# Block sums in place, fewer converted blocks and new step points in a one-core attention and bilinear-GLU kernel

## The chip, the cores and the metric

The kernel runs on one core of one Trainium2 chip. The metric is the device time of one execution in microseconds (us); lower is better. The core has five engines that run their own instruction queues: TensorE (PE, with its weight loads shown apart as PEld), VectorE (DVE), ScalarE (ACT), GpSimd (POOL) and SyncE (SP), whose queue here issues the DMA transfers.

## The reference

Input x has 2048 rows of 576 float32 numbers. All of it, cut to what matters:

```
xn = layernorm(x)
s  = attention(xn, wqkv, wo)      # 32 heads of 18, causal, window of 256
h  = (xn @ w_gate) * (xn @ w_up)  # 576 -> 4608, no nonlinearity
g  = silu(h @ w_down)             # 4608 -> 576
return x + s * g
```

## The kernel before

**Numbers in two halves.** Each float32 operand of a matmul is scaled and split into a float16 high part and a float16 low part. `hi` (line 190) makes the high part on ACT, `lo` (line 193) the low part on DVE. A product takes three matmuls: high by high, high by low, low by high.

**Seven products for eight.** The gate and up products of a group of F are done by a scheme of seven block products (Strassen's kind). A group `g` covers 256 columns of F, as F tile 0 and F tile 1 of 128 each; a chunk `c` is 512 rows of x, as two halves of 256. K (576) is four blocks of 128 and a tail of 64, block 4. The weights of gate and up (`kind` 0 and 1) come as raw float32 tiles `RAW[g, kind]` of 5 K blocks by 256 columns. `t_sum` (lines 494 to 507, on POOL) forms the differences of weight blocks that the scheme needs into a float32 tile `tf`; `t_hi` and `t_lo` split them into the float16 tile `tw`, one for each kind and each pair of sums. `up_hi` and `up_lo` split the plain blocks into `upw` tiles (`UW[g, k]`: k is 0 and 1 for F tile 0 of gate and up, 2 and 3 for F tile 1). `wd_sum`, `wd_hi` and `wd_lo` do the tail difference. `s_steps` forms the sums of x blocks once for each chunk, before and during the first slots.

**Slots and places.** There are 18 groups by 4 chunks, 72 slots: slot 4g + c does chunk c of group g. A slot has 16 places. At each place PE gets some matmuls of the seven products (`seven_place`, line 1160), and then every step that the table `AT` puts at that place is issued, in that order, to its engine. Nothing reorders an engine's queue afterwards, so the table is the order of the work. Places of a group's weight steps count from slot 4g - 4, the first slot of the group before: 0 to 15 lie in that slot, 48 to 63 in slot 4g - 1, and 64 and above in slot 4g itself, the first that uses the weights.

A slot's products come in the order 0, 2, 1, 3, 4, 5, 6. Product 2 (from place 2 of the slot) and 3 read `tw` of pair 0, products 4 (from place 9) and 5 read `tw` of pair 1, product 6 (from place 14) reads F tile 1. Results go from PSUM to SBUF on ACT and DVE (`gt`, lines 1126 and 1130); `seven_mult` (line 1135) multiplies gate by up on POOL (`ht`) or DVE; `h_hi` and `h_lo` (lines 1002 and 1008) split the product into `hh`; `down` (line 1024), one slot later, multiplies by w_down, and DVE adds it to `acc` (line 1031).

**Attention** for two heads of one chunk runs beside it in slots 1 to 64: `score_pairs` (PE), `score` (DVE, line 908), `shifted` and `probs` (ACT, lines 916 to 923), `turn_probs` (line 929: a subtraction on POOL or DVE as the table `en` says, then a transposing DMA from `pp` to `pt`), `weigh` (PE, line 941), `finish`, and a store. In slots 1 to 16 (chunk 0) there are fewer key blocks.

**Buffers.** `up_ring` gives six `upw` tiles, four a group; `tw` has four, `tf` two (also used by `ffn_spread_in`, which brings a scale back over all partitions, and by `s_steps`); `wd` one; `dn_ring` four.

**Raw loads** (`ffn_raw`) go out on SP's queue, on which the attention's loads and transposes stand too. `ffn_amax` finds the largest value (ACT squares, line 315), `ffn_spread_out`, `ffn_spread_in` and `ffn_scale` make the scale that the conversions need.

Of the kernel before, what the change touches and what calls it, by code (L numbers as in the profile page):

```python
# [8 lines left out]
F32 = mybir.dt.float32  # L9
# [11 lines left out]
def kernel(  # L21
# [43 lines left out]
    C_OUT = 1.0 / (XS * PROJ * WTOP * WTOP)  # L65
    LEAST, MOST = 2.0 ** -60, 2.0 ** 60

    AT = {"amax": (19, 20, 6),
           "dn": ((41, 45), (51, 52), (52, 48)),
           "down": ((6, 9, 12, 15, 20), (6, 8, 11, 14, 16), (6, 8, 11, 14, 16), (6, 9, 12, 15, 19)),  # L70
           "en": ((0, 1, 0, 0, 0, 0, 1, 0, 0, 0), (0, 1, 0, 0, 0, 0, 1, 0, 0, 0),
                  (0, 1, 0, 0, 0, 0, 1, 0, 0, 0), (0, 1, 0, 0, 0, 0, 1, 0, 0, 0)),
           "end": ((30, 32, 35), (28, 32, 33), (28, 32, 33), (28, 32, 33)),
           "eng": (1, 1, 0, 1, 1, 0, 1, 0, 0, 0, 0, 0, 0, 1),
           "g0": (-22, -19, -22, -21, -9, -16, -14, -11, -11),
           "h": (((15, 17), (18, 21)), ((15, 17), (19, 21)), ((15, 17), (21, 21)), ((15, 17), (19, 21))),
           "load": (8, 3, 15),
           "mult": {1: 6, 4: 18, 5: 1, 6: 0},
# [12 lines left out]
           "pairs": (6, 13),  # L91
           "raw": (8, 9, 12, 16, -6, 0),
           "scale": (26, 28, 35, 51),
           "sum": ((30, 36, 50, 59, 64), (41, 53, 56, 61, 62)),
# [5 lines left out]
           "t_hi": ((57, 57), (67, 69)),  # L100
           "t_lo": ((57, 58), (70, 71)),
           "u0": ((-9, -8, -7, -7), (-7, -7, -7, -4)),
           "up_hi": (36, 36, 60, 61),
           "up_lo": (41, 40, 65, 62),
           "wd": ((55, 56), (65, 69), (70, 74)),
           "wd0": ((-4, 3), (-1, 4), (-1, 7))}

    ctx.enter_context(tc.manual_schedule())
    const = ctx.enter_context(tc.tile_pool(name="const", bufs=1))
# [22 lines left out]
    sig = const.tile([128, 4], F32, name="sig")  # L132

    def up_ring():
        return ring.tile([128, 10, 128], F16, name="upw", bufs=6)

    def dn_ring():
        return ring.tile([128, 3, D], F16, name="dnw", bufs=4)
# [50 lines left out]
    def hi(w, rv, s):  # L189
        nc.scalar.activation(w, rv, AF.Copy, scale=s)  # L190
# [165 lines left out]

    def qk_split(m):
        if m < QM:
            w = UW["q", m] = up_ring() if m < 6 else pro.tile([128, 10, 128], F16, name=f"wq{m}")
# [76 lines left out]
    def ffn_spread_in(g):  # L436
        if g == 0:
            SC[g, "sp"] = spread_in(f"f{g}", pro, 3)
            return
        t = sums.tile([128, 2, 2, 128], F32, name="tf", bufs=2).rearrange("p a b n -> p (a b n)")  # L440
        t = t[:, 0:384].rearrange("p (a n) -> p a n", n=3)
# [12 lines left out]
    def ffn_scale2(g):  # L454
# [2 lines left out]
        nc.gpsimd.tensor_scalar(sc[:, 9:10], sc[:, 9:10], C_FFN * (FTOP / 2) ** 3, None, op0=OP.mult)  # L457
        nc.gpsimd.tensor_tensor(sc[:, 9:10], sc[:, 9:10], sc[:, 5:6], op=OP.mult)

    def up_hi(g, k):  # L460
        if (g, k) not in UW:
            UW[g, k] = up_ring()
        w = UW[g, k]
        hi(w[:, 0:5], RAW[g, k % 2][:, :, k // 2 * 128:k // 2 * 128 + 128], SC[g][:, 6 + k % 2:7 + k % 2])

    def up_lo(g, k):
        w = UW[g, k]
        lo(w[:, 5:10], RAW[g, k % 2][:, :, k // 2 * 128:k // 2 * 128 + 128], SC[g][:, 6 + k % 2:7 + k % 2],
           w[:, 0:5])

    TF, TW, SX, XD, WD = {}, {}, {}, {}, {}


    def wd_part(g, kind, i):
        if g not in WD:
            WD[g] = ring.tile([128, 2, 2, 128], F16, name="wd", bufs=1)
        return WD[g][:, i, kind]  # L480

    def wd_sum(g, kind):
        r = RAW[g, kind][:, 4]
# [10 lines left out]
    def t_sum(g, kind, n):  # L494
        r = RAW[g, kind].rearrange("p k (f n) -> p k f n", f=2)
        b = {(k, f): r[:, 2 * k:2 * k + 2, f] for k in range(2) for f in range(2)}
        if n == 0:
            if g == 0:
                TF[g, kind] = rqk.rearrange("p k n -> p (k n)")[:, 1024 * kind:1024 * kind + 1024] \
                    .rearrange("p (a k n) -> p a k n", a=4, k=2)  # L500
            else:
# [5 lines left out]
        nc.gpsimd.tensor_tensor(t[:, to], x0, x1, op=OP.subtract)  # L507

    def t_part(g, kind, pair):
        t = TF[g, kind]  # L510
        return t[:, 2 * pair:2 * pair + 2] if g == 0 else t
# [13 lines left out]
    def s_steps(c):  # L525
# [13 lines left out]
        def do(e, to, x, y, f):  # L539
            if to in ("w", "z") and to not in t:  # L540
                if c < 2:
                    o = 2048 + 512 * c + 2048 * (to == "z")
                    t[to] = rqk.rearrange("p k n -> p (k n)")[:, o:o + 512].rearrange("p (a n) -> p a n", a=2)
                else:
                    t[to] = sums.tile([128, 2, 2, 128], F32, name="tf", bufs=2).rearrange("p a b n -> p a (b n)")
# [487 lines left out]
    for g in range(NG):  # L1033
# [36 lines left out]

    def seven_unit(g, c, q):
        for kind in range(2):
            w1, w2 = UW[g, kind], UW.get((g, 2 + kind))
            w, k = {0: (w1, 0), 1: (w1, 2), 6: (w2, 2)}.get(q, (None, 0))
            if w is not None:
                wh, wl = w[:, k:k + 2], w[:, 5 + k:7 + k]
# [19 lines left out]
    TAIL = (1, 2, 5, 6)  # L1096

    def seven_tail(g, c, q, kind):
        w = UW[g, 2 * (q != 1) + kind]
        if q == 6:  # L1100
            return w[:, 4], XD[c], w[0:64, 9], XD[c][0:64]
        t = slice(c * 512 + (q != 1) * 256, c * 512 + (q != 1) * 256 + 256)
        if q == 1:
            return w[:, 4], XT[:, 4, t], w[0:64, 9], XT[0:64, 4, t]
        wh, wl = (w[:, 4], w[64:128, 9]) if q == 2 else (wd_part(g, kind, i)[64 * i:] for i in range(2))
        return wh, XT[:, 4, t], wl, XT2[64:128, t]


# [217 lines left out]
```

## Time and profile before

| what | value |
|---|---|
| times of the runs | 1577.73, 1577.39 and 2633.92 us; median 1577.73 |
| span of the profiled execution, first to last instruction | 1575.8 us |
| median less that span | 1.9 us |
| granted TensorE clock, mean | 1.000 |
| PE busy | 1555.8 us, 99% |
| DVE, ACT, POOL busy | 80%, 68%, 54% |
| matmuls | 15498 |

The third run stands apart from the other two and is used for nothing. The profile is of one execution. "Busy" is the union of an engine's instructions; matmuls overlap one another, so a busy PE may still lose time between their starts. In a row of a group of instructions stand the line of the code, the engine, the operation, the output and inputs by their names in the program, the shapes, the count, the busy time, the mean of one in ns, and the idle time of the engine just before them. A row of waits names who waited, for whom, how long in all, how often, and the longest. The chain of work that ended last is followed back from the last instruction, at each step to what released it.

### The profile page before, as it was taken

The numbers are of one execution on the slowest core, as the hardware profiler recorded it, in microseconds if no ns is written. First come the engines' busy times: TensorE is split into PE (matmuls) and PEld (weight loads), VectorE is DVE, ScalarE is ACT, GpSimd is POOL, SyncE is SP. The second block draws the span as 40 slices with busy tenths as digits, with TensorE's granted clock in tenths as the row PEclk, the third lists the DMA queues.
The fourth block names the chain that finished last, engine by engine and source line by source line (L and its number), as shares of the span: only waits on it lengthen the run. The fifth ranks groups of instructions, "written<-read, shape, count | busy, mean of one in ns | idle before, by whom it ended". The sixth has DMA issues, their size and how long they took to land.

```text
span 1575.8 us, 40062 instructions
## 1 busy us (share of the span) xinstructions
PE 1555.8 (99%) x15498; PEld 1106.1 (70%) x15498; DVE 1268.4 (80%) x2756; ACT 1069.8 (68%) x1854; POOL 850.8 (54%) x1066
## 2 busy tenths in 40 slices
PE   8999999999999999999999999999999999999999
PEld 5465577777777777777777777777777777777767
DVE  6537688888888988898989888888888888877654
ACT  6535477777777878777778777878778787752230
POOL 4116455656465757575766666566757575742100
PEclk9999999999999999999999999999999999999999
DMA  8683436555557676777777677767696877651338
GB/s 221 200 249 129 164 73 135 100 127 108 121 107 139 126 148 127 144 139 139 139 129 156 119 148 125 155 119 150 118 154 128 152 124 148 120 103 33 68 83 219
DMA packets 566575, 212.14 MB, mean 135 GB/s; under 512 B 504560, under 2 KB 544624, under 8 KB 566384
## 3 DMA queue, kind: packets, MB, share of 16 engines
q1 hardware_dynamic: 566384, 209.58, 64.3%
q8 instruction: 121, 1.98, 0.6%
q14 instruction: 70, 0.57, 0.1%
HBM read 76.63 MB, written 29.00 MB: 67 GB/s over the span
## 4 chain that ended last, share of the span: by engine, by line
PE 86%; DVE 6%; POOL 2%; DMA 2%; issue 1%; ACT 1%; SPq 0%; DVEq 0%; POOLq 0%; ACTq 0%
PE up L1160 41%; PE dn L1024 22%; PE pv L941 4%; PE s L387 4%; PE up L1113 3%; PE s L897 2%; PE s L1024 2%; PE s L1263 2%; PE up L1263 2%; PE up L387 1%; DVE hh L1008 1%; DMA pt<-pp 1%; PE s L338 1%; POOL pp L929 1%; DVE tw L193 1%
## 5 line engine op out<-in xcount | busy, mean ns | idle before, releaser
L1024 PE MATMUL dn<-dnw,hh 128*128 128x512 f16 (+1 forms) x3168 | 444.7, 286 | 1.1
L1160 PEld LDWEIGHTS <-tw 128*128 128x128 f16 x3456 | 319.2, 97 | 63.5 <-DVE tw L193 6.0
L1024 PEld LDWEIGHTS <-hh 128*128 128x128 f16 x3456 | 222.4, 98 | 169.2 <-issue 19.2
L1160 PEld LDWEIGHTS <-upw 128*128 128x128 f16 x3024 | 283.9, 98 | 64.5 <-issue 22.2
L1130 DVE SCALAR_TENSOR_TENSOR gt<-up,gt 128x512 f32<-128x512 f32 x360 | 247.6, 688 | 60.7 <-PE up L1113 40.1
L1031 DVE SCALAR_TENSOR_TENSOR acc<-dn,sc,acc 128x512 f32<-128x512 f32 x310 | 215.2, 694 | 99.1 <-PE dn L1024 99.1
L1160 PE MATMUL up<-XT,upw 128*128 128x256 f16 x2160 | 276.6, 273 | 0.0
L916 ACT ACTIVATE mx<-mx,sig 128x2 f32<-128x2 f32 x256 | 98.0, 383 | 212.7 <-DVE mx L908 212.7
L1160 PE MATMUL up<-XT,tw 128*128 128x256 f16 x1728 | 234.8, 272 | 3.4 <-DVE gt L1130 3.4
L1160 PE MATMUL up<-sx,tw 128*128 128x256 f16 x1728 | 224.7, 272 | 2.6 <-DVE tw L193 2.5
L1135 POOL TENSOR_TENSOR ht<-gt 128x512 f32<-128x512 f32 x72 | 92.1, 1279 | 93.1 <-DVE gt L1130 92.3
L941 PEld LDWEIGHTS <-pt 128*128 128x128 f16 x2880 | 109.7, 96 | 38.1 <-DMA pt<-pp 3.0
L941 PE MATMUL pv<-vt,pt 128*128 128x37 f16 x2880 | 112.9, 179 | 1.9 <-DMA pt<-pp 1.9
L1160 PE MATMUL up<-sx,upw 128*128 128x256 f16 x864 | 112.7, 273 | 0.0
L1126 ACT ACTIVATE gt<-up 128x512 f32<-128x512 f32 x144 | 83.6, 581 | 30.8 <-PE up L1160 17.3
L1002 ACT ACTIVATE hh<-ht 128x512 f16<-128x512 f32 x72 | 45.2, 627 | 67.4 <-POOL ht L1135 67.4
L507 POOL TENSOR_TENSOR tf<-raw 128x256 f32<-128x256 f32 x102 | 83.5, 818 | 0.1
L507 POOL TENSOR_TENSOR tf<-raw,tf 128x256 f32<-128x256 f32 x68 | 62.0, 913 | 21.7 <-DVE tw L193 21.7
L193 DVE SCALAR_TENSOR_TENSOR upw<-raw,sc,upw 128x640 f16<-128x640 f32 x72 | 71.7, 998 | 0.0
L315 ACT ACTIVATE upw<-raw 128x1280 bf16<-128x1280 f32 (+1 forms) x51 | 62.5, 1226 | 5.9 <-DMA raw<-in_B_w_up_dram 5.6
L193 DVE SCALAR_TENSOR_TENSOR tw<-tf,sc,tw 128x512 f16<-128x512 f32 x68 | 49.4, 749 | 14.5 <-ACT tw L190 13.7
L897 PE MATMUL s<-ks,qs 54*128 54x384 f16 (+2 forms) x512 | 60.2, 312 | 0.0
(1355 smaller groups left out, 2921.8 us busy)
## 6 DMA issues: line engine op xcount, KB each, us to landing
raw<-in_B_w_down_dram SPq DMA_DIRECT2D x36, 288.0 KB
qk_d<-qp SPq DMA_DIRECT2D x18, 512.0 KB
raw<-in_B_w_gate_dram SPq DMA_DIRECT2D x36, 256.0 KB
raw<-in_B_w_up_dram SPq DMA_DIRECT2D x36, 256.0 KB
ks<-qk_d SPq DMA_DIRECT2D x96, 81.0 KB
qs<-qk_d SPq DMA_DIRECT2D x128, 54.0 KB
vt<-v_d SPq DMA_DIRECT2D x48, 111.0 KB
qk_d<-qp SPq DMA_DIRECT2D x20, 256.0 KB
```

The lines of the kernel that those rows point to most:

```text
L193: nc.vector.scalar_tensor_tensor(w, rv, s, h, op0=OP.mult, op1=OP.subtract)
L387: nc.tensor.matmul(ps, a, b, start=i == 0 and not opened, stop=i == 12 and opened)
L507: nc.gpsimd.tensor_tensor(t[:, to], x0, x1, op=OP.subtract)
L897: nc.tensor.matmul(ps[:, :hi_ - lo_], QS[s][r, i * 128:(i + 1) * 128], KS[s][r, lo_:hi_], start=True, stop=True)
L916: nc.scalar.activation(mx[:, 1], mx[:, 0], AF.Identity, bias=sig[:, 2:3], scale=sig[:, 1:2])
L941: nc.tensor.matmul(PVB[s][:, j, i, :VW], pt[:, nb * j + n + n // nb * nb], VT[s][:, lo_ + n % nb, j * VW:(j + 1) * VW], start=n == 0, stop ...
L1024: nc.tensor.matmul(to, a, b, start=q == 0, stop=q == len(l) - 1)
L1031: nc.vector.scalar_tensor_tensor(d, src, SC[g][:, 9:10], d, op0=OP.mult, op1=OP.add)
L1126: nc.scalar.activation(seven_new(sl, name), CH[q], AF.Copy, scale=H_SC)
L1130: nc.vector.scalar_tensor_tensor(seven_new(sl, name), CH[q], H_SC, x, op0=OP.mult, op1=OP.add)
L1135: eng.tensor_tensor(HT[sl, f], u[:, 0], u[:, 1], op=OP.mult)
L1160: nc.tensor.matmul(CH[q][:, o], a, b, start=CH["first"], stop=last and q not in (1, 2, 5), skip_group_check=q in ON)
```

## The change

- `t_sum`, for every group but the first, writes its sums into the raw tiles themselves instead of `tf`. Four subtractions for each kind do it where there were five (one was formed twice because `tf` held two at a time). `t_part` reads them there.
- F tile 1 (`UW[g, 2]` and `UW[g, 3]`) is converted in K blocks 2, 3 and 4 alone, 384 columns instead of 640; the scheme reads no others. It has a ring of its own, `up_ring2`, of five smaller tiles; `up_ring` has four.
- `tw` has five tiles instead of four. `tf` is gone: `ffn_spread_in` takes a tile of `up_ring2`, and `s_steps` two tiles of `dn_ring`.
- The low part of the tail difference (`wd_lo`) goes into an unused half column block of `UW[g, kind]`; `wd` holds the high part alone.
- The table `AT` puts steps at new places: among others the sums at 43 to 59 (30 to 64 before), `t_hi` at 54, 57, 58, 65 (57, 57, 67, 69), `t_lo` at 58, 59, 64, 70 (57, 58, 70, 71), `up_hi` of F tile 1 at 45 and 45 (60, 61), its `up_lo` at 50 and 55 (65, 62), the raw loads of gate and up at 11, 11, 12, 13 (8, 9, 12, 16), the conversions of w_down, the scale, and some attention steps. In `en`, DVE takes the subtraction of one more half pair in slots 4g + 1, and in slots 4g + 3 the second half of pair 2 in place of the first. In `on`, three steps of `s_steps` change engine.

The diff, cut to its core:

```diff
-    AT = {"amax": (19, 20, 6),
-           "dn": ((41, 45), (51, 52), (52, 48)),
-           "en": ((0, 1, 0, 0, 0, 0, 1, 0, 0, 0), (0, 1, 0, 0, 0, 0, 1, 0, 0, 0),
-                  (0, 1, 0, 0, 0, 0, 1, 0, 0, 0), (0, 1, 0, 0, 0, 0, 1, 0, 0, 0)),
-           "raw": (8, 9, 12, 16, -6, 0),
-           "scale": (26, 28, 35, 51),
-           "sum": ((30, 36, 50, 59, 64), (41, 53, 56, 61, 62)),
-           "t_hi": ((57, 57), (67, 69)),
-           "t_lo": ((57, 58), (70, 71)),
-           "up_hi": (36, 36, 60, 61),
-           "up_lo": (41, 40, 65, 62),
-           "wd": ((55, 56), (65, 69), (70, 74)),
...
+    AT = {'amax': (20, 20, 13),
+          'dn': ((45, 45), (48, 56), (54, 46)),
+          'en': ((0, 1, 0, 0, 0, 0, 1, 0, 0, 0), (0, 1, 0, 0, 0, 1, 1, 0, 0, 0), (0, 1, 0, 0, 0, 0, 1, 0, 0, 0),
+                 (0, 1, 0, 0, 0, 0, 0, 1, 0, 0)),
+          'raw': (11, 11, 12, 13, -9, 2),
+          'scale': (24, 26, 36, 51),
+          'sum': ((43, 46, 54, 57), (48, 48, 57, 59)),
+          't_hi': ((54, 57), (58, 65)),
+          't_lo': ((58, 59), (64, 70)),
+          'up_hi': (38, 37, 45, 45),
+          'up_lo': (39, 40, 50, 55),
+          'wd': ((59, 55), (66, 73), (72, 74)),
...
     def up_ring():
-        return ring.tile([128, 10, 128], F16, name="upw", bufs=6)
+        return ring.tile([128, 10, 128], F16, name="upw", bufs=4)
+
+    def up_ring2():
+        return ring.tile([128, 6, 128], F16, name="upv", bufs=5)
...
+    def up_raw(g, k):
+        return RAW[g, k % 2][:, 0 if k < 2 else 2:5, k // 2 * 128:k // 2 * 128 + 128]
...
     def up_hi(g, k):
         if (g, k) not in UW:
-            UW[g, k] = up_ring()
-        w = UW[g, k]
-        hi(w[:, 0:5], RAW[g, k % 2][:, :, k // 2 * 128:k // 2 * 128 + 128], SC[g][:, 6 + k % 2:7 + k % 2])
+            UW[g, k] = up_ring() if k < 2 else up_ring2()
+        hi(up_parts(g, k)[0], up_raw(g, k), SC[g][:, 6 + k % 2:7 + k % 2])
...
     def t_sum(g, kind, n):
...
-                TF[g, kind] = sums.tile([128, 2, 2, 128], F32, name="tf", bufs=2)
-        t = TF[g, kind]
-        T0, T1, T3, T2 = (2, 1, 0, 3) if g == 0 else (0, 1, 0, 1)
-        to, x0, x1 = ((T0, b[0, 1], b[0, 0]), (T1, b[1, 1], t[:, T0]), (T3, b[1, 1], b[0, 1]),
-                      (T2, b[1, 0], t[:, T1]), (T0, b[0, 1], b[0, 0]))[n]
-        nc.gpsimd.tensor_tensor(t[:, to], x0, x1, op=OP.subtract)
...
+        else:
+            to, x0, x1 = ((b[0, 0], b[0, 1], b[0, 0]), (b[0, 1], b[1, 1], b[0, 1]), (b[1, 1], b[1, 1], b[0, 0]),
+                          (b[1, 0], b[1, 0], b[1, 1]))[n]
+        nc.gpsimd.tensor_tensor(to, x0, x1, op=OP.subtract)
...
-        w = TW[g, kind, pair] = sums.tile([128, 2, 2, 2, 128], F16, name="tw", bufs=4)
+        w = TW[g, kind, pair] = sums.tile([128, 2, 2, 2, 128], F16, name="tw", bufs=5)
...
-            for n in range(5):
+            for n in range(4):
                 at(b, AT["sum"][kind][n], t_sum, g, kind, n)
```

More of the change, by code (lines that the diff above doesn't have):

```diff
@@ L358, in qk_split @@
         if m < QM:
-            w = UW["q", m] = up_ring() if m < 6 else pro.tile([128, 10, 128], F16, name=f"wq{m}")
+            w = UW["q", m] = up_ring() if m < 4 else pro.tile([128, 10, 128], F16, name=f"wq{m}")
             r = rqk[:, :, m * 128:(m + 1) * 128]
@@ L439, in ffn_spread_in @@
             return
-        t = sums.tile([128, 2, 2, 128], F32, name="tf", bufs=2).rearrange("p a b n -> p (a b n)")
-        t = t[:, 0:384].rearrange("p (a n) -> p a n", n=3)
+        t = up_ring2().rearrange("p a n -> p (a n)").bitcast(F32).rearrange("p (a n) -> p a n", n=3)
         nc.sync.dma_start(t, SD[f"f{g}"].partition_broadcast(128))
@@ L458, in ffn_scale2, with up_parts @@
         nc.gpsimd.tensor_tensor(sc[:, 9:10], sc[:, 9:10], sc[:, 5:6], op=OP.mult)
+    def up_raw(g, k):
+        return RAW[g, k % 2][:, 0 if k < 2 else 2:5, k // 2 * 128:k // 2 * 128 + 128]
+    def up_parts(g, k):
+        w = UW[g, k]
+        n = 5 if k < 2 else 3
+        return w[:, 0:n], w[:, n:2 * n]
     def up_hi(g, k):
         if (g, k) not in UW:
-            UW[g, k] = up_ring()
-        w = UW[g, k]
-        hi(w[:, 0:5], RAW[g, k % 2][:, :, k // 2 * 128:k // 2 * 128 + 128], SC[g][:, 6 + k % 2:7 + k % 2])
+            UW[g, k] = up_ring() if k < 2 else up_ring2()
+        hi(up_parts(g, k)[0], up_raw(g, k), SC[g][:, 6 + k % 2:7 + k % 2])
     def up_lo(g, k):
[L467 to L474, printed above, removed]
+        h, l = up_parts(g, k)
+        lo(l, up_raw(g, k), SC[g][:, 6 + k % 2:7 + k % 2], h)
+    TF, TW, SX, XD, WD, WZ = {}, {}, {}, {}, {}, {}
     def wd_part(g, kind, i):
+        if i:
+            return UW[g, kind][:, 9]
         if g not in WD:
-            WD[g] = ring.tile([128, 2, 2, 128], F16, name="wd", bufs=1)
-        return WD[g][:, i, kind]
+            WD[g] = ring.tile([128, 2, 128], F16, name="wd", bufs=1)
+        return WD[g][:, kind]
     def wd_sum(g, kind):
@@ L544, in do @@
                 else:
-                    t[to] = sums.tile([128, 2, 2, 128], F32, name="tf", bufs=2).rearrange("p a b n -> p a (b n)")
+                    if not WZ:
+                        for q in ("w", "z"):
+                            WZ[q] = dn_ring().rearrange("p a n -> p (a n)")[:, 0:1024].bitcast(F32) \
+                                .rearrange("p (a n) -> p a n", a=2)
+                    t[to] = WZ[to]
             x, y = (t[q] if isinstance(q, str) else a(*q) for q in (x, y))
@@ L1098, in seven_tail @@
     def seven_tail(g, c, q, kind):
-        w = UW[g, 2 * (q != 1) + kind]
-        if q == 6:
-            return w[:, 4], XD[c], w[0:64, 9], XD[c][0:64]
         t = slice(c * 512 + (q != 1) * 256, c * 512 + (q != 1) * 256 + 256)
         if q == 1:
+            w = UW[g, kind]
             return w[:, 4], XT[:, 4, t], w[0:64, 9], XT[0:64, 4, t]
-        wh, wl = (w[:, 4], w[64:128, 9]) if q == 2 else (wd_part(g, kind, i)[64 * i:] for i in range(2))
+        w = UW.get((g, 2 + kind))
+        if q == 6:
+            return w[:, 2], XD[c], w[0:64, 5], XD[c][0:64]
+        wh, wl = (w[:, 2], w[64:128, 5]) if q == 2 else (wd_part(g, kind, i)[64 * i:] for i in range(2))
         return wh, XT[:, 4, t], wl, XT2[64:128, t]
```

39 lines of the change are left out of this document (21 added, 18 removed), and 34 rows, old and new, of the table AT.

## The prediction

> **What bounds the kernel now.** I read the parts of the page first, then the waits of PE, then the chain that ended last, then the work of each engine slot by slot, and at the end one slot instruction by instruction.
>
> ```profile
> span 1575.8 us, 40062 instructions
> PE 1555.8 (99%) x15498; PEld 1106.1 (70%) x15498; DVE 1268.4 (80%) x2756; ACT 1069.8 (68%) x1854; POOL 850.8 (54%) x1066
> ```
>
> ```profile
> PE up L1160 <- DVE gt L1130: 3.4, 4, 2.1
> PE up L1160 <- DVE tw L193: 2.5, 8, 0.4
> PE pv L941 <- DMA pt<-pp: 1.9, 3, 1.1
> ```
>
> PE is busy for 99% of the span, and the diff adds or removes no matmul. So PE's own work is a floor, and only its waits can go. The list of waits names three of over 1.5 us in the main loop (3.4, 2.5 and 1.9 us). A pipelined matmul hides a short wait inside its 272 ns, so I measure the waits by the pace of the slots instead. The chain that ended last has a block of 36 matmuls that starts at a fixed point of a slot:
>
> ```profile
> 430.44 3.93 PE up L1160 x36
> 448.62 3.93 PE up L1160 x36
> ...
> 503.36 3.93 PE up L1160 x36
> 522.01 3.93 PE up L1160 x36
> ...
> 1335.65 3.93 PE up L1160 x36
> ...
> 1376.80 1.94 DVE hh L1008 x2
> ```
>
> Early, a slot takes 448.62 - 430.44 = 18.18 us and four take 503.36 - 430.44 = 72.92, which is 4 x 18.18 = 72.72 plus 0.2. Later a slot takes 522.01 - 503.36 = 18.65 us, so a group of four should take 74.60. But the eleven groups from 503.36 to 1335.65 take 832.29 against 11 x 74.60 = 820.60: 11.69 us are lost. Which slot loses them, and who is full there (columns: start and end, length, PE, PEld, DVE, ACT, POOL; the slots 4g+1, 4g+2, 4g+3 and the next 4g, cut at the same place):
>
> ```profile
> 789.82:808.47 18.65, 18.65 (x212) 13.72 (x209) 14.13 (x33) 14.02 (x25) 10.66 (x13) 1.00 0.88 137
> 808.47:827.12 18.65, 18.65 (x206) 13.72 (x205) 16.64 (x40) 14.99 (x26) 12.30 (x16) 1.00 0.64 117
> 827.12:845.77 18.65, 18.65 (x206) 13.71 (x205) 16.26 (x36) 14.94 (x26) 14.51 (x19) 1.00 0.64 138
> 845.77:865.39 19.62, 19.20 (x205) 13.55 (x204) 18.66 (x38) 15.46 (x27) 11.22 (x14) 1.00 0.90 165
> ```
>
> The first slot of a group loses it: 19.62 - 18.65 = **0.97 us, once in each late group**. DVE has 18.66 us of work there, for a slot that PE could do in 18.65. Eleven groups make 10.67 of the 11.69; 1.0 us is irregular. The row at 1376.80 above is a DVE piece of the chain that I find below in slot 4g, so a twelfth group pays too: 12 x 0.97 = 11.64. In that stretch the chain leaves PE for DVE:
>
> ```profile
> 845.90 1.10 DVE pp L929
> 847.00 1.94 DVE hh L1008 x2
> ...
> 851.74 0.75 DVE tw L193
> ...
> 855.69 1.29 PE dn L1024 x6
> ```
>
> PE's own rows in order of time show what each wait costs:
>
> ```profile
> 847.66 1.75 PE L1024 MATMUL dn<-dnw,hh 128*128 128x512 f16 x6
> 849.25 0.61 PE L941 MATMUL pv<-vt,pt 128*128 128x37 f16 x18
> ...
> 853.49 0.38 PE L1160 MATMUL up<-sx,tw 128*128 128x256 f16 x2
> 854.17 0.61 PE L1160 MATMUL up<-sx,tw 128*128 128x256 f16 x4 [0.31 <-DVE tw L193]
> 854.77 0.60 PE L1160 MATMUL up<-XT,tw 128*128 128x256 f16 x4
> ```
>
> And the first hh step of four slots (min/median/max in ns), with the POOL row that stands beside the slow one:
>
> ```profile
> L1008 DVE SCALAR_TENSOR_TENSOR hh<-hh,ht x4: 679/682/1398, 827.7 to 884.7; 128x512 f16<-128x512 f16 x4
> ```
>
> ```profile
> 846.54 1.23 POOL L929 TENSOR_TENSOR pp<-sm__13372,pp 128x384 f16<-128x384 f32 x1
> ```
>
> First, six down matmuls start at 847.66 and the next work at 849.25: 1.59 us, against 1.29 for six that wait for nothing (855.69). They wait 0.30 us for hh, because DVE does its pp subtraction first (845.90) and then needs 1.40 us for an hh step that takes 0.68 in the other slots. Second, matmuls step by 3.93 / 36 = 0.109 us; two from 853.49 should be followed at 853.71, and the next starts at 854.17: 0.46 us for tw of kind 1. Third, four from 854.17 end at 854.61, and the next starts at 854.77: 0.16 us for gt, late behind the same tw. Together 0.92 of the 0.97.
>
> **The change part by part.** The rows that price it are groups over eleven late groups:
>
> ```profile
> L193 DVE SCALAR_TENSOR_TENSOR upw<-raw,sc,upw 128x640 f16<-128x640 f32 x44 | 43.1, 979 | 0.0
> ...
> L193 DVE SCALAR_TENSOR_TENSOR tw<-tf,sc,tw 128x512 f16<-128x512 f32 x44 | 32.0, 749 | 12.9 <-ACT tw L190 12.6
> L507 POOL TENSOR_TENSOR tf<-raw 128x256 f32<-128x256 f32 x66 | 56.1, 850 | 0.0
> L190 ACT ACTIVATE upw<-raw,sc 128x640 f16<-128x640 f32 x44 | 34.0, 819 | 0.0
> ```
>
> *Sums in place.* Per group two of ten POOL subtractions go, 2 x 0.85 = 1.7 us; the other eight keep their size. POOL is busy 10.7 to 14.5 us in a slot of 18.65, so this alone is worth nothing to PE. New waits: a sum now overwrites raw, so it must follow the conversions that read raw. up_lo stands at places 39, 40, 50 and 55, the sums that write the same blocks at 43, 48, 54 and 57: two to eight places, at some 1.2 us each (18.65 / 16). DVE would have to be over 2 us late in the third and fourth slots, where it has 2 us to spare, before POOL stood, with pp, o and the ht product queued behind it. I cost it at nothing; without that cover it is the second rival.
>
> *F tile 1 in three blocks.* Four of the 640-wide conversions per group become 384 wide. A 384-wide one is an estimate between nothing saved and 384/640 of the row: DVE 0.59 to 0.98, ACT 0.49 to 0.82; I take 0.6 for both, near the lower end on DVE because 512 wide (the tw row) takes 0.749. DVE loses 2 x 0.38 = 0.8 us a group. More counts that they leave the crowded end: up_lo goes from places 65 and 62 to 50 and 55. The third slot then has on DVE 16.26 - 2 x 0.98 + 2 x 0.6 = 15.5, and takes a tw step (0.75): 16.3 us, as full as before.
>
> *Spare buffers.* A fifth tw buffer and a ring of their own for F tile 1 are what lets t_hi of pair 1 go from places 67 and 69 to 58 and 65, and t_lo from 70 and 71 to 64 and 70. So one tw step (0.75, at 851.74) leaves DVE's chain altogether, and the other has its ACT step five places ahead. wd_lo of kind 0 goes from 70 to 72, behind both, which I leave uncounted. The tw conversions of places 57 and 58 take buffers that the last matmuls of the group before leave by place 57, so ACT may stand there for one place (1.2 us), with eight places left until PE reads at 66.
>
> *The pp that stood ahead of hh.* The table swaps which half of a pair DVE subtracts, so in the fourth slot's tail (executed in slot 4g) hh of the first F tile comes ahead of DVE's pp (1.10) and the second hh behind it.
>
> The chain on DVE ahead of the late tw so loses 0.75 and, if hh takes 0.68 again, 0.7: 1.45 us where 0.92 is needed. All three waits should fall. What is late next is the second hh: it is needed for the sixth down matmul at 847.66 + 5 x 0.215 = 848.74, and DVE would come to it at about 845.90 + 0.68 + 1.10 = 847.68 and end at 848.36 if nothing stretches, 849.1 if one of the three steps is stretched by the 0.7 seen above. That leaves between 0 and 0.4 us per group; I take 0.15, 12 x 0.15 = 1.8 us.
>
> The slow hh (it begins when pp ends, at about 847) ends 0.6 us after POOL's pp, which ends at 846.54 + 1.23 = 847.77: as if DVE stood until POOL was done and then ran its 0.68. The Trainium skill says so (SBUF — State Buffer, "Who interferes with whom"): a VectorE instruction with two SBUF inputs and a GpSimd one that reads SBUF exclude each other, and the second blocks until the first ends. By that rule the swap puts POOL's half of pp at place 19, directly beside hh, and hh is blocked again.
>
> *The rest.* ACT gets two 0.6 us conversions and one dnw (0.77) more at place 45:
>
> ```profile
> 894.76 0.77 ACT L190 ACTIVATE dnw<-raw,sc 128x576 f16<-128x576 f32 x1
> 897.40 0.39 ACT L916 ACTIVATE mx<-mx,sig 128x2 f32<-128x2 f32 x1 [1.87 <-DVE mx L908]
> ```
>
> That is 1.97 us, and ACT stands idle for 1.87 just there; without that gap it would push back the probabilities behind it by as much. One pp more (1.10) goes to DVE in slot 4g+1, whose 14.13 us are the lightest; if PE had to wait for it, it would be 12 x 1.10 = 13.2 us. The eight raw loads move from places 8, 9, 12, 16 to 11, 11, 12, 13 on SP's queue: nearer to the transposes of places 12 and 13, whose results are used from place 21 on, nine places or 10 us later. Start: PE's 3.4 us for gt (the longest 2.1) stand almost all in slot 0, behind DVE steps that keep their places, so they stay.
>
> **Sum.** 11.64 goes, 1.8 comes back, the irregular 1.0 us and the start stay: 9.8 us less. The span of the profiled execution, 1575.8, becomes 1566.0; the median of the runs shown, 1577.73, lies 1.93 above the span, so I forecast 1577.7 - 9.8 = 1567.9.
>
> **The rivals.**
> *The wait only moves.* hh is stretched again by POOL's pp beside it, at both steps, and PE waits the 0.4 us computed above plus the tw wait in part (0.3): 0.7 x 12 = 8.4 stay where I count 1.8: 1567.9 + 6.6 = 1574.5, at the worst all, 1578. For it: the 1.40 row. Against it: DVE has 0.75 us less ahead of tw even so. The Trainium skill's rule above (SBUF — State Buffer) is this rival's mechanism.
> *The table doesn't bring tw earlier.* Sums wait in POOL's queue for up_lo, and tw is as late as before; the 0.46 and 0.16 stay: 12 x 0.62 = 7.4 back, 1567.9 + 7.4 = 1575.3. Against it: places two to eight apart.
> *Slower: transposed probabilities late.* The raw loads at 11 now wait on SP for wd_lo of place 72, two places later, and the transposes stand behind them in one queue. The decision falls where a transpose lands after PE reaches place 21 or 22. The longest such wait seen is 1.1 us (the pv row above). In each of 16 attention groups that is 17.6 us: 1567.9 + 17.6 = 1585.5. Against it: only three such waits in the whole run now.
>
> **How the numbers follow.** Forecast, 1562 to 1573: 0.64. The first two rivals, 1573 to 1580: 0.24. Slower, 1580 and above: 0.09. Below 1562, the irregular waits and the start's gone as well (11.64 + 1.0 + 3.4 = 16.0): 0.03. The range 1562 to 1580 leaves out 0.12. A measurement of this kernel can tell 2%, 31.6 us, from no change; no case reaches 1546 because PE's work is the floor, and 1609 would take over two late transposes in each slot 4g; what I don't see gets the rest: faster 0.01, same 0.97, slower 0.02.
>
> **What would show it.** Right: the block of 36 matmuls returns every 74.6 to 74.8 us late in the kernel; DVE's work in slot 4g is about 17.2 us; the rows of PE waiting for tw are gone; POOL has eight sums per group. Wrong: 75.3 or more per group, with hh still at 1.4 us beside a POOL step (first rival), POOL standing for upw ahead of its sums (second), or PE waiting for pt in every group (third).

## The result, and the profile after

The changed kernel takes 1565.12 us (median of four runs, 1565.05 to 1565.64), beside 1577.56 for the kernel before on the same chip: a ratio of 0.9922, with a 95% interval of 0.9907 to 0.9937. That is 12.4 us less; the forecast was 9.8 less, 1567.9. By 2% it counts as the same time, as expected; the interval shows that the gain is real.

The page after, its span and busy times:

```profile
span 1563.3 us, 40073 instructions
PE 1550.1 (99%) x15498; PEld 1107.8 (71%) x15498; DVE 1259.1 (81%) x2773; ACT 1061.9 (68%) x1854; POOL 796.5 (51%) x1015
```

The span is 12.5 us shorter (1575.8 before). The shares of PE hardly move, 99% to 99%: they don't show a loss of 0.8%. POOL has lost 54 us of work and DVE 9. The two longest waits of PE in the main loop:

```profile
PE up L1176 <- DVE gt L1146: 3.4, 4, 2.1
PE pv L956 <- DMA pt<-pp: 0.7, 1, 0.7
```

The row of PE waiting for tw is gone. The 3.4 us of gt at the start are unchanged. From the chain that ended last, the block of 36 matmuls at its fixed point of a slot (start, length):

```profile
502.53 3.93 PE up L1176 x36
...
577.13 3.93 PE up L1176 x36
...
726.33 3.93 PE up L1176 x36
...
767.74 6.35 DMA pt<-pp
...
801.76 3.93 PE up L1176 x36
...
1324.12 3.93 PE up L1176 x36
...
1398.07 3.93 PE up L1176 x36
```

A late group now takes 577.13 - 502.53 = 74.60 us, exactly four slots of 18.65. The eleven groups take 1324.12 - 502.53 = 821.59 against the floor of 820.60, so 0.99 is left where 11.69 was. Of that, 801.76 - 726.33 = 75.43 holds 0.83, in the one group in which the chain goes through a late transpose (767.74), the 0.7 of the list of waits.

The whole 12.5 us can be booked with these rows and the same rows of before. The first block is 503.36 - 502.53 = 0.83 earlier; the eleven groups give 832.29 - 821.59 = 10.70; the twelfth, 1398.07 - 1324.12 = 73.95 against 1410.57 - 1335.65 = 74.92 (the next such block of before's chain), gives 0.97; and from there to the end both kernels take 165.23. The sum is 12.50.

Three slots, 4g+1, 4g+3 and the next 4g (columns: start and end, length, PE, PEld, DVE, ACT, POOL):

```profile
786.03:804.53 18.50, 18.50 (x205) 13.57 (x203) 14.59 (x34) 13.67 (x24) 8.51 (x10) 1.00 0.75 120
...
823.18:841.82 18.64, 18.64 (x206) 13.67 (x205) 17.74 (x39) 14.61 (x26) 15.35 (x21) 1.00 0.68 133
841.82:860.62 18.80, 18.80 (x208) 13.83 (x207) 16.10 (x38) 14.53 (x26) 9.28 (x11) 1.00 0.93 185
```

DVE's work in slot 4g fell from 18.66 to 16.10 us, in slot 4g+3 it rose from 16.26 to 17.74. The cut is at a fixed time here, so 18.50 and 18.80 together are two slots of 18.65; the 0.97 is gone.

What the fourth slot's tail does in slot 4g, DVE's rows in order of time, and POOL's subtractions around it:

```profile
839.10 0.69 DVE L1151 TENSOR_TENSOR gt<-gt 128x512 f32<-128x512 f32 x1
839.70 1.40 DVE L196 SCALAR_TENSOR_TENSOR tw<-raw,sc,tw 128x512 f16<-128x512 f32 x1
...
841.79 0.68 DVE L1023 SCALAR_TENSOR_TENSOR hh<-hh,ht 128x512 f16<-128x512 f16 x1
842.39 0.55 DVE L944 TENSOR_TENSOR pp<-sm__13343,pp 128x384 f16<-128x384 f32 x1
```

```profile
839.43 1.13 POOL L944 TENSOR_TENSOR pp<-sm__13343,pp 128x384 f16<-128x384 f32 x1 [0.38 <-ACT pp L938]
844.21 0.91 POOL L944 TENSOR_TENSOR pp<-sm__13347,pp 128x384 f16<-128x384 f32 x1 [3.65 <-ACT pp L938]
```

hh comes ahead of pp, as forecast. POOL's half ends at 840.56 and its next begins at 844.21, so neither hh nor pp has a POOL step beside it: hh takes 0.68, pp 0.55. The tw step of place 64 is now in front of this tail, where it takes 1.40 us beside POOL and nobody waits. In the kernel before, a POOL sum stood just there, the fifth one of place 64 (POOL's row, then DVE's):

```profile
845.86 0.73 POOL L507 TENSOR_TENSOR tf<-raw 128x256 f32<-128x256 f32 x1
```

```profile
845.88 1.12 DVE L929 TENSOR_TENSOR pp<-sm__13372,pp 128x384 f16<-128x384 f32 x1
846.92 1.40 DVE L1008 SCALAR_TENSOR_TENSOR hh<-hh,ht 128x512 f16<-128x512 f16 x1
```

DVE's pp begins with that sum and takes 1.12 us for 0.55; POOL's own pp (846.54, 1.23) follows the sum, and hh takes 1.40 beside it. So the 0.30 us that PE waited for hh came from two stretched steps in a row, and the first of them goes back to the sum. Eight of the eleven late groups are like this one; in the other three pp comes just ahead of the sum and takes 0.55, and hh takes 1.21.

### The profile page after: what moved, and what is told of

Same layout as the page of the kernel before. It is cut to its first block, busy times and chain, and to the rows that moved or that the text cites. A ratio compares the mean times of both kernels' runs of the same rounds, so it can differ in the third digit from the quotient of the medians.

```text
span 1563.3 us, 40073 instructions
## 1 busy us (share of the span) xinstructions
PE 1550.1 (99%) x15498; PEld 1107.8 (71%) x15498; DVE 1259.1 (81%) x2773; ACT 1061.9 (68%) x1854; POOL 796.5 (51%) x1015
## 4 chain that ended last, share of the span: by engine, by line
PE 95%; DVE 1%; ACT 1%; DMA 0%; issue 0%; SPq 0%; DVEq 0%
PE up L1176 46%; PE dn L1039 25%; PE pv L956 5%; PE s L390 4%; PE up L1129 3%; PE s L912 2%; PE s L1039 2%; PE s L1279 2%; PE up L1279 2%; PE up L390 1%; PE s L341 1%; PE pv L390 1%; PE dn L390 1%; PE up L341 0%; DMA pt<-pp 0%; PE dn L341 0%
## 5 line engine op out<-in xcount | busy, mean ns | idle before, releaser
L1176 PE MATMUL up<-XT,upw 128*128 128x256 f16 x1872 | 238.6, 273 | 0.0
L1176 PEld LDWEIGHTS <-upw 128*128 128x128 f16 x1872 | 178.2, 98 | 27.0 <-issue 0.2
L956 PEld LDWEIGHTS <-pt 128*128 128x128 f16 x2880 | 114.5, 96 | 41.8 <-DMA pt<-pp 1.6
L1176 PEld LDWEIGHTS <-upv 128*128 128x128 f16 x1152 | 105.6, 98 | 37.2 <-issue 22.0
L517 POOL TENSOR_TENSOR raw<-raw 128x256 f32<-128x256 f32 x136 | 116.6, 857 | 24.7 <-DVE upv L196 16.7
L956 PE MATMUL pv<-vt,pt 128*128 128x37 f16 x2880 | 117.8, 179 | 0.7 <-DMA pt<-pp 0.7
L1176 PE MATMUL up<-sx,upv 128*128 128x256 f16 x864 | 112.6, 273 | 0.0
L196 DVE SCALAR_TENSOR_TENSOR tw<-raw,sc,tw 128x512 f16<-128x512 f32 x68 | 67.9, 999 | 0.0
L193 ACT ACTIVATE tw<-raw,sc 128x512 f16<-128x512 f32 x68 | 46.8, 712 | 27.9 <-POOL raw L517 27.9
```

Of the source, the lines that this page charges most:

```text
L196: nc.vector.scalar_tensor_tensor(w, rv, s, h, op0=OP.mult, op1=OP.subtract)
L517: nc.gpsimd.tensor_tensor(to, x0, x1, op=OP.subtract)
L956: nc.tensor.matmul(PVB[s][:, j, i, :VW], pt[:, nb * j + n + n // nb * nb], VT[s][:, lo_ + n % nb, j * VW:(j + 1) * VW], start=n == 0, stop ...
L1176: nc.tensor.matmul(CH[q][:, o], a, b, start=CH["first"], stop=last and q not in (1, 2, 5), skip_group_check=q in ON)
```

## The experiments

Each kernel is timed in rounds beside the kernel before, and its trace is read by the same two rows, the blocks of 36 matmuls at about 503 and 1330: their distance less 820.60 is the kernel's **excess**, 11.69 for the kernel before and 0.99 for the changed one. "Regular" is the part that returns in every group; the rest is single late transposes and the like. The kernel before had a median of 1576.87, 1578.08 and 1578.74 in the three sessions, so the times below are compared by their ratios to it.

**The order of pp and hh, undone in the changed kernel.**

```diff
-                 (0, 1, 0, 0, 0, 0, 0, 1, 0, 0)),
+                 (0, 1, 0, 0, 0, 0, 1, 0, 0, 0)),
```

> The changed kernel with the row of en for slots 4g+3 as before, so that DVE's half of pp stands ahead of hh again; nothing else. Theory of places: the wait of the down matmuls for hh comes back, 12 x 0.30 = 3.6 us, 1568.7. Theory of load (the two POOL sums and the two wide conversions that left the start of slot 4g made the room): POOL is done with its half before hh, hh takes 0.68 us in either order, and the time stays at 1565.1 within 0.7.

Measured: 1564.37 us, ratio 0.992 (0.9905 to 0.9935). The chain:

```profile
502.76 3.93 PE up L1176 x36
...
1323.36 3.93 PE up L1176 x36
```

The excess is 0.00. The swapped order is worth nothing once the rest of the change is there.

**The tw steps of pair 1, back at their old places.**

```diff
-          't_hi': ((54, 57), (58, 65)),
-          't_lo': ((58, 59), (64, 70)),
+          't_hi': ((54, 57), (67, 69)),
+          't_lo': ((58, 59), (70, 71)),
```

> The changed kernel with t_hi and t_lo of pair 1 at their places of before (67, 69 and 70, 71); nothing else. Theory of places: the waits for tw and for gt behind it come back, 12 x (0.46 + 0.16) = 7.4 us, 1572.5. Theory of load: DVE is ahead by the conversions that left, so at most 2 us come back, 1565.1 to 1567.

Measured: 1571.05 us, ratio 0.9962 (0.9947 to 0.9977). The chain, PE's longest wait in the main loop (its row over the late groups), and one such wait among PE's rows:

```profile
502.55 3.93 PE up L1176 x36
...
1329.50 3.93 PE up L1176 x36
```

```profile
PE up L1176 <- DVE gt L1146: 3.9, 11, 0.4
```

```profile
850.57 0.82 PE L1176 MATMUL up<-sx,tw 128*128 128x256 f16 x6
851.75 0.92 PE L1176 MATMUL up<-XT,tw 128*128 128x256 f16 x7 [0.36 <-DVE gt L1146]
```

The excess is 6.35, of which 11 x 0.52 = 5.7 is regular: the first slot of each group is 0.52 too long. PE waits for gt once in every group, and no row of it waits for tw; in DVE's queue gt stands behind the late tw steps. So the earlier tw steps earn 0.52 a group here, by letting gt come in time.

**Both undone.**

```diff
-                 (0, 1, 0, 0, 0, 0, 0, 1, 0, 0)),
+                 (0, 1, 0, 0, 0, 0, 1, 0, 0, 0)),
-          't_hi': ((54, 57), (58, 65)),
-          't_lo': ((58, 59), (64, 70)),
+          't_hi': ((54, 57), (67, 69)),
+          't_lo': ((58, 59), (70, 71)),
```

> The two edits before together, in the changed kernel. Theory of places: 12 x 0.92 = 11.0 us come back, 1576.1, nearly the kernel before, although the sums in place, the narrow conversions and the lighter POOL stay. Theory of load: under 4 us come back, below 1569.

Measured: 1571.35 us, ratio 0.9965 (0.9953 to 0.9978), excess 5.94, regular 0.52 again. With late tw the order is worth nothing either. The time lies between the two theories. And 0.97 - 0.52 = 0.45 of each group's gain stays although both are undone.

**DVE's old load at the crowded end put back:** two conversions 640 wide, at places 65 and 62, into a tile that nobody reads afterwards.

```diff
+    def lo_more(g, kind):
+        to = EXTRA[g][:, 0:640].rearrange("p (k n) -> p k n", k=5)
+        lo(to, RAW[g, kind][:, :, 0:128], SC[g][:, 6 + kind:7 + kind], UW[g, kind][:, 0:5])
...
+            at(b, (65, 62)[kind], lo_more, g, kind)
```

> The changed kernel with two more DVE conversions per group, 640 wide, at places 65 and 62, where the ones of F tile 1 stood before; their output goes to a tile that nobody reads, so the result is untouched. Theory of places: DVE's place order at the start of slot 4g holds hh and tw early enough, so 1565 to 1567. Theory of load: these 2 x 0.9 us are the room that was made, and 5 us or more come back, 1570 and above.

Measured: 1567.57 us, ratio 0.9941 (0.9926 to 0.9956). The excess is 2.69: 11 x 0.09 = 1.0 regular, the rest single waits for pt (1.5 us in three waits). Neither theory holds: it costs more than nothing and far less than 5 us.

**POOL's old load put back:** two subtractions 256 wide, at places 64 and 62.

```diff
+    def t_fifth(g, kind):
+        r = RAW[g, kind].rearrange("p k (f n) -> p k f n", f=2)[:, 0:2]
+        to = EXTRA[g].bitcast(F32)[:, 0:256].rearrange("p (k n) -> p k n", k=2)
+        nc.gpsimd.tensor_tensor(to, r[:, :, 1], r[:, :, 0], op=OP.subtract)
...
+            at(b, (64, 62)[kind], t_fifth, g, kind)
```

> The changed kernel with one more POOL subtraction for each kind, 256 elements wide, at places 64 and 62, where the fifth sums stood before; the output goes to a tile that nobody reads. Theory of places: 1565.1 within 1. Theory of load, POOL's part: POOL's half of pp comes later and lies beside hh again, hh is stretched from 0.68 to 1.40 us, and 12 x 0.30 = 3.6 us come back, 1568.7.

Measured: 1566.23 us, ratio 0.9929 (0.9915 to 0.9944). The excess is 1.38, none of it regular. The two sums less are worth nothing by themselves.

**The order alone, in the kernel before.**

```diff
-                  (0, 1, 0, 0, 0, 0, 1, 0, 0, 0), (0, 1, 0, 0, 0, 0, 1, 0, 0, 0)),
+                  (0, 1, 0, 0, 0, 0, 1, 0, 0, 0), (0, 1, 0, 0, 0, 0, 0, 1, 0, 0)),
```

> The kernel before with the one entry of en changed for slots 4g+3 (hh ahead of DVE's half of pp); nothing else. Theory of places: the 0.30 us of hh go in each late group, 1577.6 - 3.6 = 1574.0. Theory of load: POOL is as late as before, its half lies beside hh, and at most 1 us is gained.

Measured: 1578.98 us, ratio 1.0005 (0.9996 to 1.0015). The regular 0.97 stays. The waits of PE:

```profile
PE pv L941 <- DMA pt<-pp: 4.8, 6, 1.2
PE up L1160 <- DVE tw L193: 1.9, 6, 0.4
```

The wait for tw is still there, and the late transposes take 4.8 us in place of 1.9. In slot 4g hh is first now, and still slow (DVE's row, then POOL's):

```profile
846.50 1.25 DVE L1008 SCALAR_TENSOR_TENSOR hh<-hh,ht 128x512 f16<-128x512 f16 x1
```

```profile
846.48 0.73 POOL L507 TENSOR_TENSOR tf<-raw 128x256 f32<-128x256 f32 x1
```

It begins together with POOL's sum of place 64, the fifth, ends 0.54 us after it, and PE gets no earlier what it waits for. The changed kernel has no such sum there.

**tw early, in the kernel before** (with the fifth sum of kind 0 ahead of it).

```diff
-           "sum": ((30, 36, 50, 59, 64), (41, 53, 56, 61, 62)),
+           "sum": ((30, 36, 50, 59, 60), (41, 53, 56, 61, 62)),
-           "t_hi": ((57, 57), (67, 69)),
-           "t_lo": ((57, 58), (70, 71)),
+           "t_hi": ((57, 57), (62, 66)),
+           "t_lo": ((57, 58), (66, 70)),
```

> The kernel before, four tw tiles and two tf tiles as they are, with the steps of pair 1 moved as far as these allow: fifth sum of kind 0 from 64 to 60, t_hi from 67 and 69 to 62 and 66, t_lo from 70 and 71 to 66 and 70. Theory of places: the waits for tw and gt go, 12 x 0.62 = 7.4 us, 1570.2, with none of the new buffers. Theory of load: DVE and POOL are as full as before, and under 2 us are gained.

Measured: 1583.43 us, ratio 1.0034 (1.0021 to 1.0047): **slower** than the kernel before, which neither theory had. Two of PE's waits, the chain over one undisturbed late group, and DVE's pp in the fourth slot's tail with POOL's beside it:

```profile
PE dn L1024 <- DVE hh L1008: 4.9, 12, 0.4
PE pv L941 <- DMA pt<-pp: 4.8, 5, 1.4
```

```profile
885.57 3.93 PE up L1160 x36
...
960.99 3.93 PE up L1160 x36
```

```profile
851.21 1.28 DVE L929 TENSOR_TENSOR pp<-sm__13373,pp 128x384 f16<-128x384 f32 x1
```

```profile
851.16 0.91 POOL L929 TENSOR_TENSOR pp<-sm__13373,pp 128x384 f16<-128x384 f32 x1
```

The row for tw is gone, as intended, and twelve waits for hh stand in its place, as many as there are late groups. The step that was moved ahead pushes the tail back, so that DVE's pp now meets POOL's, takes 1.28 us, and hh behind it is late. But this isn't where the kernel loses: an undisturbed late group takes 960.99 - 885.57 = 75.42, a regular 0.82 to 0.84 where the kernel before has 0.97. The loss lies elsewhere. The four early groups, from the first such block of the chain on, take 505.21 - 212.36 = 292.85 against 503.36 - 212.16 = 291.20, 1.65 more; and of the excess, 1340.85 - 505.21 - 820.60 = 15.04, about 6 us are irregular where it was 1.0, most of them late transposes (4.8 us of waits for pt against 1.9). Why the transposes are late more often was not found.

**Both, in the kernel before.**

```diff
-                  (0, 1, 0, 0, 0, 0, 1, 0, 0, 0), (0, 1, 0, 0, 0, 0, 1, 0, 0, 0)),
+                  (0, 1, 0, 0, 0, 0, 1, 0, 0, 0), (0, 1, 0, 0, 0, 0, 0, 1, 0, 0)),
-           "sum": ((30, 36, 50, 59, 64), (41, 53, 56, 61, 62)),
+           "sum": ((30, 36, 50, 59, 60), (41, 53, 56, 61, 62)),
-           "t_hi": ((57, 57), (67, 69)),
-           "t_lo": ((57, 58), (70, 71)),
+           "t_hi": ((57, 57), (62, 66)),
+           "t_lo": ((57, 58), (66, 70)),
```

> The two edits of the kernel before together: table entries alone, no buffer, no sum in place, no narrow conversion. Theory of places: 11.0 us gained, 1566.6, nearly the changed kernel. Theory of load: under 3 us gained.

Measured: 1583.0 us, ratio 1.0034 (1.0022 to 1.0046), excess 1340.49 - 503.90 - 820.60 = 16.0. The fourth slot's tail, on DVE and on POOL:

```profile
849.84 1.42 DVE L1008 SCALAR_TENSOR_TENSOR hh<-hh,ht 128x512 f16<-128x512 f16 x1
```

```profile
849.80 0.90 POOL L929 TENSOR_TENSOR pp<-sm__13373,pp 128x384 f16<-128x384 f32 x1
```

This is the first rival to the letter: hh, now ahead of DVE's pp, stands beside POOL's pp and takes 1.42 us. In the changed kernel POOL's pp begins 841.79 - 839.43 = 2.36 us ahead of hh, and is over in time. The two steps that the forecast lived on, made alone, lose about 5 us (0.34% of 1577.6). As in the run before, a regular late group is a little shorter than in the kernel before (0.82 for 0.97), and the loss lies in the early groups (503.90 - 211.03 = 292.87, 1.67 more) and in single waits, 5.5 us of them for pt. What turns the two steps into a gain of 0.97 must be in the rest of the change.

**All four undone in the changed kernel:** order, tw places, and both loads back (the sums here go into the last tw tile of the group before, which is free then).

```diff
-                 (0, 1, 0, 0, 0, 0, 0, 1, 0, 0)),
+                 (0, 1, 0, 0, 0, 0, 1, 0, 0, 0)),
-          't_hi': ((54, 57), (58, 65)),
-          't_lo': ((58, 59), (64, 70)),
+          't_hi': ((54, 57), (67, 69)),
+          't_lo': ((58, 59), (70, 71)),
...
+            at(b, (64, 62)[kind], t_fifth, g, kind)
+            at(b, (65, 62)[kind], lo_more, g, kind)
```

> The changed kernel with all four things of before at the start of slot 4g at once: DVE's pp ahead of hh, t_hi and t_lo of pair 1 at 67 to 71, two 640-wide DVE conversions at 65 and 62, two POOL subtractions at 64 and 62 (the last two into tiles that nobody reads, so the result is untouched). If these four are the whole of the gain in the late groups, a late group takes 75.5 us again instead of 74.6 and the time is 1576 to 1577. If something else in the change (the new ring, fewer waits for loads, the other places) carries part, it stays below 1574.

Measured: 1572.1 us, ratio 0.9957 (0.9943 to 0.9972), excess 6.57, regular 0.52, the same as with tw late alone. The loads cost nothing when tw is late. PE doesn't wait for hh in the late groups of this run. Yet hh takes 1.40 us in each of them, beside POOL's pp (844.54, 1.23); it is in time because DVE's pp ahead of it takes 0.57 to 0.60. POOL's fifth sum is all but over when that pp begins, and ends 0.17 us later (POOL's row, then DVE's):

```profile
843.26 1.31 POOL L530 TENSOR_TENSOR tw<-raw 128x256 f32<-128x256 f32 x1
```

```profile
844.40 0.59 DVE L957 TENSOR_TENSOR pp<-sm__13373,pp 128x384 f16<-128x384 f32 x1
844.92 1.40 DVE L1036 SCALAR_TENSOR_TENSOR hh<-hh,ht 128x512 f16<-128x512 f16 x1
```

**Order and both loads back, tw early.**

```diff
-                 (0, 1, 0, 0, 0, 0, 0, 1, 0, 0)),
+                 (0, 1, 0, 0, 0, 0, 1, 0, 0, 0)),
...
+            at(b, (64, 62)[kind], t_fifth, g, kind)
+            at(b, (65, 62)[kind], lo_more, g, kind)
```

> The same without the late tw steps: tw stays early, while the order of pp and hh and both loads of DVE and POOL are as before. Theory of order and load together: the wait for hh (0.30 us a group, a stretched hh of 1.40 us beside POOL's pp) is back, and only that: 12 x 0.30 to 0.45, 1568.7 to 1570.5. If order and load carry nothing while tw is early, it stays within 1 of 1565.1.

Measured: 1574.8 us, ratio 0.9978 (0.9969 to 0.9987). The wait of PE, and DVE and POOL in the fourth slot's tail of a regular group:

```profile
PE dn L1052 <- DVE hh L1036: 3.2, 14, 0.5
```

```profile
921.95 1.35 DVE L196 SCALAR_TENSOR_TENSOR upv<-raw,sc,upw 128x640 f16<-128x640 f32 x1
...
923.61 0.87 DVE L957 TENSOR_TENSOR pp<-sm__14705,pp 128x384 f16<-128x384 f32 x1
924.41 0.68 DVE L1036 SCALAR_TENSOR_TENSOR hh<-hh,ht 128x512 f16<-128x512 f16 x1
```

```profile
922.57 1.50 POOL L957 TENSOR_TENSOR pp<-sm__14705,pp 128x384 f16<-128x384 f32 x1
```

The excess is 1332.89 - 505.40 - 820.60 = 6.89, 0.41 a group regular, as the first theory says; the time is above both. PE waits for hh again: the wide conversion stands behind tw and ahead of the tail and takes 1.35 us, DVE's pp (0.87) then ends behind POOL's, and hh, itself 0.68, comes late. In two of the eleven groups the second hh also meets a subtraction of POOL and takes 1.43.

Beside the run before, the sole difference is the place of the tw steps: 1574.8 us for early against 1572.1 for late. In the late groups early is not the worse (0.41 regular against 0.52). Of the 2.6 us between the two spans 1.1 lie ahead of the first block, 1.2 in the four early groups (505.40 - 212.59 = 292.81 against 503.03 - 211.45 = 291.58) and 0.3 in the excess. So with the old loads and the old order the early tw is worth 0.11 a group where it is worth 0.52 without them, and this is lost again elsewhere.

**Order and DVE's load back, POOL's left out, tw early.**

```diff
-                 (0, 1, 0, 0, 0, 0, 0, 1, 0, 0)),
+                 (0, 1, 0, 0, 0, 0, 1, 0, 0, 0)),
...
+            at(b, (65, 62)[kind], lo_more, g, kind)
```

> The same without POOL's two subtractions: order of pp and hh as before, the two wide DVE conversions back, tw early, POOL as light as in the changed kernel. If DVE's load makes hh late, it is as slow as the kernel with both loads back, 1568.7 to 1570.5. If POOL's sums make it, through the stretched hh, it is at 1565 to 1567 and no hh row is over 0.75 us.

Measured: 1567.64 us, ratio 0.9929 (0.9912 to 0.9945). The excess is 1328.43 - 504.06 - 820.60 = 3.77, 0.1 a group regular, as with DVE's load alone; hh never takes over 0.69. So with the order and DVE's load back it is the two POOL sums that make hh late: each of the three alone is worth 0 to 0.09, order and DVE's load 0.1, all three 0.41. Both loads without the order, and the order with the sums alone, were not run, so the order's part in the 0.41 is not shown.

**The start made lighter:** in slot 0, the two low halves of the first group's w_down and six of the steps that form the sums of x for chunk 2 come later. This one aims at the 3.4 us of gt that neither kernel touches.

```diff
-                 (-13, -11, -11, -9, -7, -7, -3, -3, 2, 3, 4, 5, 6, 4, 6, 7, 14),
+                 (-13, -11, -11, -9, -7, -7, -3, -3, 2, 3, 8, 9, 10, 8, 9, 10, 14),
...
-            at(b, AT["dn"][1][k] if g else 65 + k, dn_lo, g, k)
+            at(b, AT["dn"][1][k] if g else 72 + k, dn_lo, g, k)
```

> The changed kernel with less on DVE at the start of slot 0, where PE still waits 3.4 us for gt: the low halves of w_down of group 0 go from places 1 and 2 to 8 and 9, and six steps of the x sums of chunk 2 from places 4 to 7 to places 8 to 11. If those steps are what gt stands behind, the 2.1 us wait of place 6 goes and 1.5 to 3 us are gained, 1562 to 1563.6. If they only push later waits, the time stays at 1565.1 within 1.

Measured: 1575.96 us, ratio 0.9982 (0.9972 to 0.9991): 10 us lost, all of it at the start. PE's longest wait, the wait of SP's queue, the POOL step that stands, and the DMA that POOL waits for, as SP issues it in the chain that ended last:

```profile
PE up L1176 <- ACT gt L1142: 6.0, 1, 6.0
```

```profile
SPq L424 <- DVE dnw L196: 10.3, 1, 10.3
```

```profile
199.59 1.16 POOL L562 TENSOR_TENSOR dnw<-XT,sx 128x512 f32<-128x512 f16 x1 [10.48 <-DMA XT<-dnw]
```

```profile
196.45 0.53 SPq L585
```

Neither theory had this. The next load of w_down (line 424) overwrites the raw tile that the moved low halves read, so SP's queue stands for them, 10.3 us where it stood 1.1 in the changed kernel. The small DMA of the x sums (line 585) is behind that load in the queue and goes out at 196.45 rather than 186.51, although what it sends was there at 189.54 (ACT's step at 189.14, 0.40). POOL stands 10.48 us for it, ACT 4.30 behind POOL's result, and gt comes 6 us late. So the w_down steps, moved to relieve DVE, held up the queue of SP.

## Why the prediction was right, and where it was not

*Where the time is lost.* Right. The loss of 0.97 us sat in slot 4g, once in each of twelve late groups, and is gone in all twelve: 10.70 and 0.97, 11.67 for the 11.64 of the sum.

*The second hh.* The term of 0.15 x 12 = 1.8 us was **mis-sized**: 0 was measured. I put pp at 1.10 us from the row of before. That was a stretched one, beside POOL's fifth sum (845.86); by itself it takes 0.55, so the second hh comes about half a microsecond sooner. hh over eleven groups (min/median/max in ns; the source line's own row):

```profile
L1023 DVE SCALAR_TENSOR_TENSOR hh<-hh,ht x44: 676/681/693, 542.6 to 1346.4; 128x512 f16<-128x512 f16 x44
```

1404 was the maximum before. This term is 1.8 of the 2.8 us between forecast and result; 0.2 is the difference of the two medians of before (1577.73 and 1577.56), and the rest, 0.83, is the earlier first block.

I take the 0.83 for scatter and not for the change: the first block of 36 matmuls of the chain begins at 212.16 before and at 211.41 after, but in the three variants of before it begins at 211.03, 211.62 and 212.36, and in the variants of after with the same start between 211.00 and 212.59.

*Which edits bring it.* **Wrong in part**, and the total hid it. I gave the swapped order 0.30 of the 0.92, by reading the row in which pp stands ahead of hh. Undone it costs nothing in the new kernel, where POOL's pp is over before DVE's begins, and made alone it gains nothing in the old one, where POOL's fifth sum stretches hh. The 0.30 goes with the time of that sum: with all four steps undone it is all but over when DVE's pp begins, and PE doesn't wait for hh although pp stands ahead of it and hh itself takes 1.40. I gave the earlier tw 0.62; it is 0.52 in the changed kernel, 0.11 with the old order and loads put back, and 0.13 to 0.15 in the old kernel, where hh then waits behind it. The failed step is "the chain on DVE loses 1.45 us where 0.92 is needed": I added up what leaves the queue ahead of tw, didn't ask what the same step does when it stands ahead of hh, and didn't ask what POOL runs beside pp.

*Sums in place, and narrow F tile 1.* I priced the subtractions at nothing, and the load's leaving as a mere 0.8 us of DVE. Each alone is worth 0 to 0.09, so those prices hold by themselves. But with the order undone the two together take most of what early tw gains, and the fifth sum at its old time is what stretches pp in the old kernel, and hh there when the order is swapped: "worth nothing" was right as a price and wrong as a statement on the change. The sizes were right (groups over some eleven late groups):

```profile
L196 DVE SCALAR_TENSOR_TENSOR tw<-raw,sc,tw 128x512 f16<-128x512 f32 x47 | 48.6, 1033 | 0.0
...
L196 DVE SCALAR_TENSOR_TENSOR upv<-raw,sc,upv 128x384 f16<-128x384 f32 x22 | 13.4, 610 | 0.0
```

0.610 us on DVE, and 0.600 in ACT's row, stand beside the 0.6 of the estimate. What I missed is that the tw steps become dearer at their new places: 1.03 us on average for 0.75.

*What stays open.* With order, tw and both loads undone, the changed kernel still gains 0.97 - 0.52 = 0.45 us a group, some 5 us. The trace of that run shows where: PE's 0.30 for hh isn't there, and PE loses 0.52 for gt where it lost 0.62 for tw and gt, together 0.40. The first comes with the POOL sum, which begins 846.19 - 843.26 = 2.93 us ahead of the tail's down matmuls, 847.66 - 845.86 = 1.80 in the kernel before. POOL has one sum less just before it (839.10, against 840.43 and 841.11 before); which of the new places does this, no run separated, so this part of the cause is read from the trace and not shown by an edit of its own. Why gt is 0.1 sooner is open too: the low part of the tail difference, which I "left uncounted", stands ahead of gt at its old place 70 as at the new 72. The fifth tw tile was not tried alone in the old kernel.

*The rivals.* The wait that only moves did not come about here, though the old kernel with order and tw changed shows its mechanism in full, and the changed one with order and both loads back shows a wait that moved to hh, by way of a stretched pp. The second rival's condition occurs, and misses PE (POOL's row, over the late groups):

```profile
L517 POOL TENSOR_TENSOR raw<-raw 128x256 f32<-128x256 f32 x90 | 75.2, 836 | 12.0 <-DVE upv L196 11.1
```

POOL stands about 1 us in each group for the conversion that reads raw, and no wait of PE follows. The third, late transposes, came once, for 0.7 us. The signs: 74.60 a group as forecast; DVE's slot 4g at 16.10 rather than 17.2, and slot 4g+3 at 17.74 rather than 16.3, since the early tw fell into that one.

## What to carry to other kernels

Where one engine is 99% busy, measure the pace of a repeated block in the chain, not the shares: 75.57 against 74.60 showed the loss and its slot, and no share did. A duration read off a crowded moment is no price: pp at 1.10 and hh at 1.40 were 0.55 and 0.68 by themselves; look at what the other engine runs beside a slow row before pricing its removal. And moving a step earlier in a full queue paid in full here only where something else had left the queue: the same move was worth 0.52 us a group with the loads gone and 0.11 to 0.15 with them there, and there it lost more in other places. Edits that cost 0 to 0.09 one at a time cost 0.41 together; such edits are tested together, and an edit is not worthless because undoing it alone costs nothing.

## What the runs showed of the hardware

Steps of DVE and POOL that read SBUF tiles stretch each other in pairs, both ways, and more widely than the rows of before had shown. Beside a POOL step, DVE's hh takes 1.25 to 1.42 us for 0.68, the tw step 1.40 for 0.75 (839.70, with POOL's pp from 839.43 to 840.56), and pp 0.87 to 1.28 for 0.55. POOL's pp at 839.43 takes 1.13 for the 0.91 of the one at 844.21: it begins inside DVE's product at 839.10 and ends 0.77 after it.

The stretches can follow one another. In the kernel before POOL's sum (845.86), DVE's pp (845.88), POOL's pp (846.54) and DVE's hh (846.92) each end 0.41, 0.77 and 0.55 after the one ahead. These are less than the undisturbed lengths, 0.55, 0.91 and 0.68, by 0.13 or 0.14; in the row at 839.70 DVE ends 0.54 after POOL, 0.21 less than its 0.75; the hh steps at 846.50 and 849.84 end 0.54 and 0.56 after POOL. The rule of the Trainium skill (SBUF — State Buffer, "Who interferes with whom"), that the second of such a pair blocks until the first ends, agrees with these rows but for 0.1 to 0.2 us: the second ends that much sooner than if it ran its whole length after the first.
